# Which queue loads what, one held load, and the order of the first matmuls in a kernel that sums a state-space layer and a feed-forward layer

## The chip, the cores and the metric

The kernel runs on one core of a Trainium2 chip. The metric is the time of one execution on the device, in microseconds (us). TensorE (PE) does the matmuls, VectorE (DVE) and ScalarE (ACT) the elementwise work, GpSimd (POOL) some small operations and a few transfers. SyncE (SP) and ScalarE issue most of the transfers (DMAs), each into a queue of its own; 16 DMA engines carry all of them.

## What is computed

```python
xn = _layernorm(x)                                   # x: [1, 2048, 512], bf16
out = x + A(xn) + B(xn)

def A(x, ...):                                       # state-space layer, P = D = 512
    Lam_bar = exp(dt * Lam)                          # dt = exp(log_dt), Lam complex
    B_bar = ((Lam_bar - 1.0) / Lam)[:, None] * Bmat
    Bu = einsum("bld,pd->blp", x, B_bar)
    h_t = Lam_bar * h_{t-1} + Bu[:, t, :]            # over 2048 steps
    return 2.0 * einsum("blp,dp->bld", h, Cmat).real + x * Dskip

def B(x, w_gate, w_up, w_down):                      # F = 1376
    return (silu(x @ w_gate) * (x @ w_up)) @ w_down
```

## The kernel before

The 2048 rows of x are 16 tiles of 128 rows (`xall[:, n, :]`, called x0, x1, ... here), in four chunks of 512 rows. For each chunk TensorE needs the normalized rows transposed, `xnT` (512 features on partitions in four blocks `k`, rows as columns). Then come three kinds of matmuls: `bproj` (L346, the input of the recurrence, weights `BT`, eight groups of four), gate and up (L421, eleven feature tiles of 128 columns, weights `wg`, `wu`), and the output (`out_ffn` L501 and `out_ssm` L510, which add into the same PSUM bank). VectorE runs the recurrence as a scan (L388) between two complex rotations; ScalarE copies matmul results out of PSUM and does the silu.

The order of instructions on each engine is written out by hand (`manual_schedule`); a small backlog (`queue`, `pump`) interleaves the VectorE work of the recurrence with the matmul groups from the second chunk on. Waits between engines follow from the data. A DMA issued from SyncE or ScalarE uses one of eight completion semaphores in turn and, in the built program, waits until the DMA that had it before has landed.

The first chunk is done in a head of its own, tile by tile, because its loads arrive one after another:

- `dummy(11, CW)`: eleven matmuls of 512 columns on a constant, whose results are not used (L569), then TensorE waits for tile 0.
- VectorE: statistics of x0 (`ln_stats(0)`, L174 and L175), statistics of x1 (L600), the normalization of tile 0 (`norm_dve(0)`, L192), the second step of the statistics of x1 (L602), and so on, in this order. The reciprocal square root of the variance comes from ScalarE as `Ln` and `Exp` (`rstd_act`, L179 and L180), for which `preload_act_table_set` loads ScalarE's table (L596).
- `xT_pe(n)`: four transposes of tile n on TensorE (L209), in two halves of two feature blocks; ScalarE (L218) or VectorE (L216) copies each half to `xnT`. It is called T(n) in the prediction. After T(0) come four short dummies of 128 columns.
- `head_mm(which, lo, hi, ks, fis)` (L592): gate (`which` = 0) or up (1) matmuls for the row tiles `lo` to `hi`, feature blocks `ks` and feature tiles `fis`; feature tiles 0 and 1 first, since the first group of weights (`wg0`, `wu0`) holds these two. The results are kept in six PSUM banks until all four row tiles of the chunk are done.

The weights of gate and up come in four groups, `wg0` to `wg3` and `wu0` to `wu3` (two, two, three and three feature tiles; `load_w1`, L112). SyncE issues x0, wg0, x2, wg1, then x4 to x7 as one load (L126), wg2, wu2, four transposing loads of B's real part (`BT`, L131), wg3, wu3, four of its imaginary part, and three pieces of the last feature tile. ScalarE issues x1, wu0, x3, wu1. GpSimd issues three small parameter rows (`prm_rows`, L125).

The last feature tile has 96 columns (1280 to 1375). `w_last` packs its 96 gate columns and 32 of its up columns into one set of 128 weights; the other 64 up columns are in `wu_last`. The gate columns stand there in the order 1312 to 1375, 1280 to 1311, and `wd_sb` holds the matching rows of `w_down` in the same order, in two loads.

In the last chunk the result is added up on VectorE (L513) and stored per tile of 128 rows from SyncE (L514); only the last tile is cut into three column blocks, two of which ScalarE stores.

Of the kernel before, what the change touches and what calls it, by code (L numbers as in the profile page):

```python
# [10 lines left out]
F32 = mybir.dt.float32  # L11
# [12 lines left out]
def kernel(  # L24
# [17 lines left out]
    nc = tc.nc  # L42
    _, L, D = A_x.shape
    Pst = A_Lambda_re.shape[0]
    F = B_w_gate.shape[1]
    assert L % 512 == 0 and D % 128 == 0 and Pst % 128 == 0 and Pst == D
    CW = 512
# [3 lines left out]
    TPC = CW // 128  # L51
    KD = D // 128
# [6 lines left out]
    LA, LB = 32, 64  # L59
    FL = (FT - 1) * 128  # L60
    assert fsz[-1] == LA + LB and NCH % 2 == 0
    EPS = 1e-5

    const = ctx.enter_context(tc.tile_pool(name="const", bufs=1))
# [14 lines left out]
    x_v = A_x[0].rearrange("(n p) d -> p n d", p=128)  # L79
    out_v = out[0].rearrange("(n p) d -> p n d", p=128)  # L80
    wg_v = B_w_gate.rearrange("(k p) f -> p k f", p=128)
    wu_v = B_w_up.rearrange("(k p) f -> p k f", p=128)


    xall = const.tile([128, NT, D], BF16, name="xall")
# [3 lines left out]
    wg_g, wu_g = [], []  # L89
# [4 lines left out]
    w_last = const.tile([128, KD, 128], BF16, name="w_last")  # L94
    wu_last = const.tile([128, KD, LB], BF16, name="wu_last")
    wd_sb = const.tile([128, FT, D], BF16, name="wd_sb")
# [7 lines left out]
    def wslice(groups, fi, k):  # L104
        for (a, b), t in zip(fgroups, groups):
            if a <= fi < b:
                return t[:, k, (fi - a) * 128:(fi - a) * 128 + fsz[fi]]


    def load_w1(q, tiles, view, gi):  # L110
        a, b = fgroups[gi]
        q.dma_start(out=tiles[gi][:], in_=view[:, :, a * 128:min(F, b * 128)])  # L112


    nc.sync.dma_start(out=xall[:, 0, :], in_=x_v[:, 0, :])
    nc.scalar.dma_start(out=xall[:, 1, :], in_=x_v[:, 1, :])
    load_w1(nc.sync, wg_g, wg_v, 0)
    load_w1(nc.scalar, wu_g, wu_v, 0)
    nc.sync.dma_start(out=xall[:, 2, :], in_=x_v[:, 2, :])
    nc.scalar.dma_start(out=xall[:, 3, :], in_=x_v[:, 3, :])  # L120
    load_w1(nc.sync, wg_g, wg_v, 1)
    load_w1(nc.scalar, wu_g, wu_v, 1)
    prm_rows = const.tile([3 * NQ, 128], BF16, name="prm_rows")
    for i, v in enumerate((A_Lambda_re, A_Lambda_im, A_log_dt)):
        nc.gpsimd.dma_start(out=prm_rows[i * NQ:(i + 1) * NQ, :], in_=v.rearrange("(q j) -> q j", j=128))  # L125
    nc.sync.dma_start(out=xall[:, TPC:2 * TPC, :], in_=x_v[:, TPC:2 * TPC, :])  # L126
    load_w1(nc.sync, wg_g, wg_v, 2)
    load_w1(nc.sync, wu_g, wu_v, 2)
    for part, src in enumerate((A_B_re, A_B_im)):
# [3 lines left out]
            load_w1(nc.sync, wg_g, wg_v, 3)  # L133
            load_w1(nc.sync, wu_g, wu_v, 3)

    nc.sync.dma_start(out=w_last[:, :, 0:LB], in_=wg_v[:, :, FL + LA:F])
    nc.sync.dma_start(out=w_last[:, :, LB:LB + LA], in_=wg_v[:, :, FL:FL + LA])
    nc.sync.dma_start(out=w_last[:, :, LB + LA:128], in_=wu_v[:, :, FL:FL + LA])

    def load_late():  # L140
        nc.sync.dma_start(out=wu_last[:], in_=wu_v[:, :, FL + LA:F])
        nc.sync.dma_start(out=xall[:, 2 * TPC:NT, :], in_=x_v[:, 2 * TPC:NT, :])
        nc.sync.dma_start(out=wd_sb[:, 0:nfull, :], in_=B_w_down[0:nfull * 128, :].rearrange("(k p) d -> p k d", p=128))
        if nfull < FT:
            nc.sync.dma_start(out=wd_sb[0:LB, nfull, :], in_=B_w_down[FL + LA:F, :])
            nc.sync.dma_start(out=wd_sb[LB:LB + LA, nfull, :], in_=B_w_down[FL:FL + LA, :])

    nfull = F // 128


    ones = nc.const_aps.tensor(1.0, (128, CW), BF16)
    neg_half = const.tile([128, TPC], F32, name="neg_half")
    nc.vector.memset(neg_half[:], -0.5)
    eps_t = const.tile([128, 1], F32, name="eps_t")
    nc.vector.memset(eps_t[:], EPS)
    ident = const.tile([128, 128], BF16, name="ident")
    make_identity(nc, ident[:])
    jidx = const.tile([128, CW], F32, name="jidx")
# [14 lines left out]
    def ln_stats(n):  # L173
        nc.vector.bn_stats(out=stats[:, n, :], in_=xall[:, n, :])  # L174
        nc.vector.bn_aggr(out=mv[:, n, :], in_=stats[:, n, :])  # L175

    def rstd_act(n):

        nc.scalar.activation(out=ve[:, n:n + 1], in_=mv[:, n, 1:2], func=ACT.Ln, bias=eps_t[:, 0:1])  # L179
        nc.scalar.activation(out=rstd[:, n:n + 1], in_=ve[:, n:n + 1], func=ACT.Exp, scale=-0.5)  # L180
# [19 lines left out]
    HK = KD // 2  # L200

    def xT_pe(n, on_dve=(), prm_too=False):

        c, i = divmod(n, TPC)
        for h in range(2):
            tp = bank((128, HK * 128 + 3 * NQ), BF16)
            for k in range(HK):
                lo = (h * HK + k) * 128
                nc.tensor.transpose(out=tp[:, k * 128:(k + 1) * 128], in_=xn_tile(c)[:, i, lo:lo + 128],  # L209
                                    identity=ident[:])  # L210
            if prm_too and h == 1:
                prm_transpose(tp[:, HK * 128:])
            dst = xnT[:, h * HK:(h + 1) * HK, n * 128:(n + 1) * 128]
            src = tp[:, 0:HK * 128].rearrange("p (k t) -> p k t", k=HK)
            if h in on_dve:
                nc.vector.tensor_copy(out=dst, in_=src)  # L216
            else:
                nc.scalar.copy(out=dst, in_=src)  # L218
        return tp[:, HK * 128:]
# [270 lines left out]
    def out_blocks(n):  # L490

        return ((0, D // 2), (D // 2, D - 128), (D - 128, D)) if n == NT - 1 else ((0, D),)
# [11 lines left out]
    def out_ssm(n):  # L504
        c, i = divmod(n, TPC)
        res = opool.tile([128, D], BF16, name="res")
        for o, (lo, hi) in zip(o_tiles[n], out_blocks(n)):
            for part in range(2):
                for q in range(NQ):
                    nc.tensor.matmul(o[:], lhsT=w_tiles[c][:, part, q, i * 128:(i + 1) * 128],  # L510
                                     rhs=CF[:, part, q, lo:hi], start=False, stop=(part == 1 and q == NQ - 1))
            if c == NCH - 1:
                V.tensor_tensor(out=res[:, lo:hi], in0=o[:], in1=xn_end[:, i, lo:hi], op=ALU.add)  # L513
                (nc.sync if hi == D else nc.scalar).dma_start(out=out_v[:, n, lo:hi], in_=res[:, lo:hi])  # L514
            else:
                nc.scalar.copy(out=res[:, lo:hi], in_=o[:])  # L516
                nc.gpsimd.dma_start(out=out_v[:, n, lo:hi], in_=res[:, lo:hi], accum_op=ALU.add)  # L517
# [49 lines left out]
    def dummy(n, cols):  # L567
        for _ in range(n):
            nc.tensor.matmul(warm[:, 0:cols], lhsT=ones[:, 0:128], rhs=ones[:, 0:cols], start=True, stop=True)  # L569
# [18 lines left out]
    def head_mm(which, lo, hi, ks, fis):  # L588

        for fi in fis:  # L590
            for k in ks:
                nc.tensor.matmul(held[fi][which][:, lo * 128:hi * 128], lhsT=wslice((wg_g, wu_g)[which], fi, k),  # L592
                                 rhs=xnT[:, k, lo * 128:hi * 128], start=(k == 0), stop=(k == KD - 1))

    allk = range(KD)
    nc.scalar.preload_act_table_set("natural_log_exp_and_others")  # L596
    dummy(11, CW)
    ln_stats(0)
    rstd_act(0)
    nc.vector.bn_stats(out=stats[:, 1, :], in_=xall[:, 1, :])  # L600
# [6 lines left out]
    ln_stats(2)  # L607

    head_mm(0, 0, 1, range(0, HK), (0, 1))
    head_mm(1, 0, 1, range(0, HK), (0, 1))  # L610
    xT_pe(1)
    rstd_act(2)
    head_mm(0, 0, 1, range(HK, KD), (0, 1))
    head_mm(1, 0, 1, range(HK, KD), (0, 1))
    nc.vector.bn_stats(out=stats[:, 3, :], in_=xall[:, 3, :])
    norm_dve(2)
# [45 lines left out]
    def out_chunk(c):  # L662

        multiply(0)
        for n in range(c * TPC, (c + 1) * TPC):
            out_ffn(n)
            pump(FT * 0.2163)
        need(f"ssm{c}")
        need("cf")
        for n in range(c * TPC, (c + 1) * TPC):  # L670
            out_ssm(n)
            pump(2 * NQ * 0.2163)
# [28 lines left out]
    spread(fwd0[8:] + back0, norm2, "ssm0", "ln2")  # L701
    queue("cf", c_ops())
    load_late()
    for fi in range(G0, FT):
        gateup_tile(0, fi)
# [60 lines left out]
```

## Time and profile before

| | us |
|---|---|
| median of 3 runs | 180.13 |
| lowest and highest | 180.0, 180.2 |
| the profiled execution, whole | 180.19 |
| its span (first to last instruction) | 178.4 |

| engine | busy us | share of the span |
|---|---|---|
| TensorE, matmuls | 174.8 | 98% |
| TensorE, weight loads (beside matmuls) | 83.4 | 47% |
| VectorE | 153.1 | 86% |
| ScalarE | 93.9 | 53% |
| GpSimd | 23.2 | 13% |

All times of the trace count from the start of the span. The 1.8 us between the span and the whole lie before and after it. A line of the timeline has the start, the duration, the engine, the line of the kernel, the operation, what it writes and reads, and in brackets how long the engine was idle before it and what ended that. A "q" behind an engine's name is its queue issuing a transfer; the landing of the transfer is listed apart, in the issues, as us from the issue. The ends of matmuls are modelled, so the distance from one start to the next tells more of a matmul's pace than its own duration. The chain of waits is followed back from the last instruction to what released each step.

### The profile page before, as it was taken

Reading aid. Unit: us, or ns where it says so; the run is one execution under the profiler, and the core shown is the slowest. Engines: PE = TensorE matmul, PEld = TensorE weight load, DVE = VectorE, ACT = ScalarE, POOL = GpSimd, SP = SyncE. Lnnn points to the kernel's source line nnn. Section 1 sums busy time; section 2 is a strip of 40 time slices with the busy share of each in tenths; the row PEclk is TensorE's granted clock in tenths of the full one; section 3 lists DMA queues with packets and bytes.
Section 4 is the critical chain, followed back from the end, with each engine's and each line's share of the span. In section 5 each row is a group of like instructions: output and inputs, shape, how many; then the busy total and the mean of one; then the engine's idle time right before and its main releaser. Section 6 shows DMA issues by size and latency. Waiting matters only on the chain.

```text
span 178.4 us, 2463 instructions
## 1 busy us (share of the span) xinstructions
PE 174.8 (98%) x918; PEld 83.4 (47%) x918; DVE 153.1 (86%) x232; ACT 93.9 (53%) x173; POOL 23.2 (13%) x29
## 2 busy tenths in 40 slices
PE   8999999999999999999999999999999999999993
PEld 2784444444444444444444444444444444444743
DVE  2889996999999999999999999999999999950033
ACT  2579795988299957022998661024866610220000
POOL 6003000000500000027200000013405000150000
PEclk9999999999999999999999999999999999999999
DMA  5998657994137400020930000007096900072012
GB/s 169 313 256 235 114 104 190 359 160 109 34 63 235 180 0 0 0 29 6 131 75 0 0 0 0 4 0 87 9 139 90 146 5 0 0 85 32 4 48 70
DMA packets 29515, 15.53 MB, mean 87 GB/s; under 512 B 18336, under 2 KB 29440, under 8 KB 29472
## 3 DMA queue, kind: packets, MB, share of 16 engines
q1 hardware_dynamic: 24416, 11.21, 27.1%
q0 software_dynamic: 3456, 3.28, 13.8%
q10 hardware_dynamic: 1632, 0.89, 1.8%
q8 instruction: 7, 0.11, 0.3%
q14 instruction: 4, 0.03, 0.1%
HBM read 8.03 MB, written 5.24 MB: 74 GB/s over the span
## 4 chain that ended last, share of the span: by engine, by line
PE 98%; DVE 0%; issue 0%
PE ps L421 36%; PE ps L501 21%; PE ps L510 16%; PE ps L346 15%; PE ps L592 3%; PE ps L569 3%; PE ps L447 2%; PE ps L457 1%; PE ps L209 1%; DVE res L513 0%; PE ps L239 0%
## 5 line engine op out<-in xcount | busy, mean ns | idle before, releaser
L501 PE MATMUL ps<-wd_sb,guT 128*128 128x512 bf16 (+3 forms) x198 | 38.8, 356 | 0.0
L421 PE MATMUL ps<-xnT,wg 128*128 128x512 bf16 x148 | 38.0, 380 | 0.0
L421 PE MATMUL ps<-xnT,wu 128*128 128x512 bf16 x148 | 38.0, 379 | 0.0
L388 DVE TENSOR_TENSOR_SCAN g<-r_t,car,u 128x512 bf16<-128x512 f32 x24 | 28.9, 1267 | 0.0
L510 PE MATMUL ps<-CF,wt 128*128 128x512 bf16 (+2 forms) x144 | 28.3, 356 | 0.0
L346 PE MATMUL ps<-xnT,BT 128*128 128x512 bf16 x128 | 28.3, 379 | 0.0
L501 PEld LDWEIGHTS <-guT 128*128 128x128 bf16 (+1 forms) x198 | 18.5, 98 | 19.9
L516 ACT CAST res<-ps 128x512 bf16<-128x512 f32 x12 | 7.0, 585 | 38.0 <-PE ps L510 38.0
L435 ACT ACTIVATE guT<-ps 128x512 bf16<-128x512 f32 x40 | 24.9, 623 | 3.5 <-PE ps L421 3.4
L436 ACT CAST u<-ps 128x512 bf16<-128x512 f32 x40 | 24.3, 607 | 3.9 <-PE ps L421 3.9
L421 PEld LDWEIGHTS <-wu 128*128 128x128 bf16 x148 | 14.5, 98 | 17.5
L421 PEld LDWEIGHTS <-wg 128*128 128x128 bf16 x148 | 14.3, 98 | 17.6 <-issue 0.8
L517 POOL DMA_DIRECT2D out_dram<-res x12 | 11.1, 998 | 86.4 <-ACT res L516 86.4
L510 PEld LDWEIGHTS <-wt 128*128 128x128 bf16 x144 | 13.4, 98 | 14.3
L346 PEld LDWEIGHTS <-BT 128*128 128x128 bf16 x128 | 12.5, 98 | 15.1
L348 ACT CAST u<-ps 128x512 bf16<-128x512 f32 x32 | 17.4, 591 | 2.8 <-PE ps L346 2.7
L513 DVE TENSOR_TENSOR res<-ps,xn_end 128x512 bf16<-128x512 f32 (+2 forms) x6 | 3.0, 514 | 14.2 <-PE ps L510 14.2
L440 DVE TENSOR_TENSOR guT<-guT,u 128x1024 bf16<-128x1024 bf16 x20 | 13.5, 681 | 0.0
L174 DVE BATCH_NORM_STATS2 stats<-xall 128x6 f32<-128x512 bf16 x14 | 9.4, 670 | 2.6 <-DMA xall<-in_A_x_dram 2.6
L356 DVE TENSOR_TENSOR pm<-u,c 128x2048 bf16<-128x2048 bf16 x8 | 9.8, 1221 | 1.2 <-ACT c L273 1.1
L184 POOL TENSOR_TENSOR rstd<-ve,neg_half 128x4 f32<-128x4 f32 x3 | 5.3, 1750 | 41.9 <-DVE ve L183 41.9
L356 DVE TENSOR_TENSOR pm<-g,c 128x2048 bf16<-128x2048 bf16 x8 | 9.7, 1218 | 0.1
(102 smaller groups left out, 159.0 us busy)
## 6 DMA issues: line engine op xcount, KB each, us to landing
out_dram<-in_A_x_dram SPq DMA_DIRECT2D x1, 1536.0 KB, 8.0
out_dram<-res POOLq DMA_DIRECT2D x12, 128.0 KB, 3.1
out_dram<-xall POOLq DMA_DIRECT2D x3, 512.0 KB, 5.7
wd_sb<-in_B_w_down_dram SPq DMA_DIRECT2D x1, 1280.0 KB, 10.6
xall<-in_A_x_dram SPq DMA_DIRECT2D x1, 1024.0 KB, 6.2
wg<-in_B_w_gate_dram SPq DMA_DIRECT2D x2, 384.0 KB, 5.6
wu<-in_B_w_up_dram SPq DMA_DIRECT2D x2, 384.0 KB, 5.4
wu<-in_B_w_up_dram ACTq DMA_DIRECT2D x2, 256.0 KB, 5.1
```

The costliest lines, as they stand in the source:

```text
L174: nc.vector.bn_stats(out=stats[:, n, :], in_=xall[:, n, :])
L346: nc.tensor.matmul(ps[:], lhsT=BT[:, part, k, q * 128:(q + 1) * 128], rhs=xnT[:, k, c * CW:(c + 1) * CW], start=(k == 0), stop=(k == KD - 1))
L348: nc.scalar.copy(out=u_tiles[c][:, part, q, :], in_=ps[:])
L356: V.tensor_tensor(out=t[:], in0=flat(src()[:, i]), in1=flat(tab[:]), op=ALU.mult)
L388: V.tensor_tensor_scan(out=g()[:, part, q, :], data0=r_t[:, q:q + 1].to_broadcast([128, CW]), data1=u_tiles[c][:, part, q, :], initial=ini ...
L421: nc.tensor.matmul(ps[:fs, lo:hi], lhsT=wslice(groups, fi, k), rhs=xnT[:, k, c * CW + lo:c * CW + hi], start=(k == 0), stop=(k == KD - 1))
L435: nc.scalar.activation(out=guT[:fs, fi, :], in_=psg[:fs], func=ACT.Silu)
L436: nc.scalar.copy(out=u_pair[c][:fs, fi % 2, :], in_=psu[:fs])
L440: products.append(lambda: V.tensor_tensor(out=g, in0=g, in1=u, op=ALU.mult))
L501: nc.tensor.matmul(o[:], lhsT=gu_tiles[c][:fsz[fi], fi, i * 128:(i + 1) * 128], rhs=wd_sb[:fsz[fi], fi, lo:hi], start=(fi == 0), stop=False)
L510: nc.tensor.matmul(o[:], lhsT=w_tiles[c][:, part, q, i * 128:(i + 1) * 128], rhs=CF[:, part, q, lo:hi], start=False, stop=(part == 1 and q ...
L517: nc.gpsimd.dma_start(out=out_v[:, n, lo:hi], in_=res[:, lo:hi], accum_op=ALU.add)
```

## The change

- SyncE issues x0, wg0, wu0, wg1, wu1; ScalarE issues x1, x2, x3. A VectorE memset writes half of x1's buffer first; the load of x1 overwrites it and so waits for it.
- The two small memsets that stood further down on VectorE, and the load of ScalarE's table, now stand ahead of these loads.
- x4 to x7 come in two loads of two tiles.
- Nine long dummies instead of eleven.
- For row tile 0, all four blocks of gate come first, then T(1), then all four blocks of up. Before, T(1) stood between blocks 0 and 1 of gate and up and blocks 2 and 3.
- The last feature tile's columns stay in order: `w_last` comes in two loads, its rows of `w_down` in one. The numbers of matmuls stay as they were.
- The first of the four stores of the last chunk is cut into two halves of 256 columns, from ScalarE and SyncE.

```diff
+    neg_half = const.tile([128, TPC], F32, name="neg_half")
+    nc.vector.memset(neg_half[:], -0.5)
+    eps_t = const.tile([128, 1], F32, name="eps_t")
+    nc.vector.memset(eps_t[:], EPS)
+
+    nc.scalar.preload_act_table_set("natural_log_exp_and_others")
+
     nc.sync.dma_start(out=xall[:, 0, :], in_=x_v[:, 0, :])
+    nc.vector.memset(xall[:, 1, 0:D // 2], 0.0)
     nc.scalar.dma_start(out=xall[:, 1, :], in_=x_v[:, 1, :])
     load_w1(nc.sync, wg_g, wg_v, 0)
-    load_w1(nc.scalar, wu_g, wu_v, 0)
-    nc.sync.dma_start(out=xall[:, 2, :], in_=x_v[:, 2, :])
+    nc.scalar.dma_start(out=xall[:, 2, :], in_=x_v[:, 2, :])
+    load_w1(nc.sync, wu_g, wu_v, 0)
     nc.scalar.dma_start(out=xall[:, 3, :], in_=x_v[:, 3, :])
     load_w1(nc.sync, wg_g, wg_v, 1)
-    load_w1(nc.scalar, wu_g, wu_v, 1)
+    load_w1(nc.sync, wu_g, wu_v, 1)
...
-    nc.sync.dma_start(out=xall[:, TPC:2 * TPC, :], in_=x_v[:, TPC:2 * TPC, :])
+    for n in (TPC, TPC + 2):
+        nc.sync.dma_start(out=xall[:, n:n + 2, :], in_=x_v[:, n:n + 2, :])
...
-    nc.sync.dma_start(out=w_last[:, :, 0:LB], in_=wg_v[:, :, FL + LA:F])
-    nc.sync.dma_start(out=w_last[:, :, LB:LB + LA], in_=wg_v[:, :, FL:FL + LA])
-    nc.sync.dma_start(out=w_last[:, :, LB + LA:128], in_=wu_v[:, :, FL:FL + LA])
+    nc.sync.dma_start(out=w_last[:, :, 0:LB + LA], in_=wg_v[:, :, FL:F])
+    nc.sync.dma_start(out=w_last[:, :, LB + LA:128], in_=wu_v[:, :, FL + LB:F])
...
-        nc.sync.dma_start(out=wu_last[:], in_=wu_v[:, :, FL + LA:F])
+        nc.sync.dma_start(out=wu_last[:], in_=wu_v[:, :, FL:FL + LB])
...
-            nc.sync.dma_start(out=wd_sb[0:LB, nfull, :], in_=B_w_down[FL + LA:F, :])
-            nc.sync.dma_start(out=wd_sb[LB:LB + LA, nfull, :], in_=B_w_down[FL:FL + LA, :])
+            nc.sync.dma_start(out=wd_sb[0:F - FL, nfull, :], in_=B_w_down[FL:F, :])
...
-                (nc.sync if hi == D else nc.scalar).dma_start(out=out_v[:, n, lo:hi], in_=res[:, lo:hi])
+                for a, b in ((0, D // 2), (D // 2, D)) if i == 0 else ((lo, hi),):
+                    (nc.sync if b == D else nc.scalar).dma_start(out=out_v[:, n, a:b], in_=res[:, a:b])
...
-    nc.scalar.preload_act_table_set("natural_log_exp_and_others")
-    dummy(11, CW)
+    dummy(9, CW)
...
     head_mm(0, 0, 1, range(0, HK), (0, 1))
-    head_mm(1, 0, 1, range(0, HK), (0, 1))
+    head_mm(0, 0, 1, range(HK, KD), (0, 1))
     xT_pe(1)
     rstd_act(2)
-    head_mm(0, 0, 1, range(HK, KD), (0, 1))
+    head_mm(1, 0, 1, range(0, HK), (0, 1))
     head_mm(1, 0, 1, range(HK, KD), (0, 1))
```

More of the change, by code (lines that the diff above doesn't have):

```diff
@@ L144, in load_late @@
         if nfull < FT:
-            nc.sync.dma_start(out=wd_sb[0:LB, nfull, :], in_=B_w_down[FL + LA:F, :])
-            nc.sync.dma_start(out=wd_sb[LB:LB + LA, nfull, :], in_=B_w_down[FL:FL + LA, :])
+            nc.sync.dma_start(out=wd_sb[0:F - FL, nfull, :], in_=B_w_down[FL:F, :])
     nfull = F // 128
     ones = nc.const_aps.tensor(1.0, (128, CW), BF16)
[L152 to L155, printed above, removed]
     ident = const.tile([128, 128], BF16, name="ident")
```

## Prediction

> **What bounds the kernel now.** I read the chain of waits first, then the timeline of the first 14 us, then the DMA issues one by one, then DMA rates by window. The chain in order of time:
>
> ```profile
> 0.78 4.85 PE ps L569 x11
> 5.63 0.31 PE ps L209 x4
> 5.94 0.23 PE ps L569 x4
> 6.17 0.04 issue
> 6.21 0.61 PE ps L592 x8
> ...
> 175.60 0.02 issue
> 175.63 0.29 DVE res L513
> ```
>
> TensorE is the chain from end to end. Past 6.21 us the idle in it is 0.02 us, so later loads, VectorE work and stores are covered, and what an edit is worth is how far it moves the start of that stream. Up to 5.63 the stream is eleven dummy matmuls (L569) that compute nothing. What releases the first real work is in the timeline:
>
> ```profile
> 0.74 0.41 ACTq L116 DMA_DIRECT2D xall<-in_A_x_dram  x1
> 0.74 0.40 SPq L115 DMA_DIRECT2D xall<-in_A_x_dram  x1
> ...
> 2.78 1.28 ACT L596 ACT_TABLE_LOAD   x1 [2.78 <-issue]
> ...
> 3.55 0.69 DVE L174 BATCH_NORM_STATS2 stats<-xall 128x6 f32<-128x512 bf16 x1 [2.65 <-DMA xall<-in_A_x_dram]
> ...
> 4.37 0.66 DVE L600 BATCH_NORM_STATS2 stats<-xall 128x6 f32<-128x512 bf16 x1
> ...
> 5.06 0.41 DVE L192 TENSOR_SCALAR xall<-xall,mv,rstd 128x512 bf16<-128x512 bf16 x1
> ...
> 5.52 0.25 PEld L209 LDWEIGHTS <-xall 128*128 128x128 bf16 x4 [0.80 <-DVE xall L192]
> ```
>
> The transposes of tile 0 wait for its normalization (L192), that for the statistics (L174), those for the landing of tile 0 (x0) at 3.5. Statistics of tile 1 (L600) stand in front of L192 on VectorE, so x1 counts too. The dummies start 0.427 us apart (last one at 5.00), so the eleventh is through at 5.43, just before L192 ends at 5.47: both edges meet. The head thus hangs on x0's landing, then on x1's. The issues that started together:
>
> ```profile
> xall<-in_A_x_dram ACTq DMA_DIRECT2D x1, 128.0 KB, 3.0
> xall<-in_A_x_dram SPq DMA_DIRECT2D x1, 128.0 KB, 2.8
> ```
>
> x0 and x1, on two queues in the same instant, land 2.8 and 3.0 us later: they share the engines. Read in the same way one by one: wg0 lands 3.7 after its issue at 1.20 (4.9), wu0 4.2 after 1.18 (5.4), x2 4.6 after 1.66 (6.3), x3 5.1 after 1.67 (6.8), wg1 5.9 after 2.21 (8.1), wu1 6.0 after 2.29 (8.3).
>
> **The change, part by part.** *x0 alone.* In the windows the engines go from 70 GB/s (2.00 to 2.25) to 324 to 336 GB/s (2.25 to 3.00). x1's 131 KB at 332 GB/s is 0.39 us of shared transfer taken out from before x0's end: x0 lands at 3.1 instead of 3.5, gain 0.39. Bounds: no gain, if x0's 2.8 us is latency and not share; at most 0.7, since the quickest load on the page from a quiet queue (wu_last, 64 KB) lands 2.1 us after issue. I take 0.39, nearest to the row of these very loads.
>
> *The hold.* x1 now waits for a memset of half of it, third on VectorE after 0.84 + 0.06. VectorE's tiny memsets take 0.06, GpSimd's 128x128 one 0.22: x1 is issued at 1.0 to 1.15. By its own row it lands 3.0 later, 4.0 to 4.15; by x0's, 2.8, 3.8 to 3.95. L600 wants it at 4.37 - 0.39 = 3.98. Loss 0 to 0.17; I take 0.05, since x1 now shares with wg0 and has nothing before it on its queue. Behind it on ScalarE's queue are x2 and x3: issued at about 1.55 and 2.0, wanted at 6.48 and 7.30 less the gain. Half the bytes ahead of them are gone (wu0 left the queue), so they should land by 5.0 and 5.8.
>
> *The table load* moves from 2.78 to the front of ScalarE, 0.75 to 2.03. It must be done by L179 (4.49, then 4.1); at the old place it ended at 4.06. Worth nothing, if it does not hold back the DMAs behind it (a rival below).
>
> *wu0 and wu1 to SyncE, gate of tile 0 first.* The PE now does gate k0 to k3 of feature tiles 0 and 1, then T(1), then up. The second half of xnT, copied by ScalarE until 6.38, is wanted at 6.43 instead of 6.88: at most 0.02 late. wu0 is now wanted at 6.83 - 0.3 = 6.5 instead of 6.38. Ahead of its end are x0 to x3, wg0 and itself, 1.05 MB. By the windows (about 611 KB by 4.0, 767 by 4.5, 897 by 5.0, 1030 by 5.5) that much is moved by 5.6; loads land 0.4 to 0.8 after their bytes (wg0 and wu0), so 6.0 to 6.4. Loss 0; if the lag is 1.2 us, as for x3, wu0 lands at 6.8 and costs 0.3. wg1 and wu1 have the same bytes ahead as before, or fewer.
>
> *Eleven dummies to nine.* The ninth ends at 0.78 + 9 x 0.427 = 4.62. It removes 0.85 us of blocking in front of transposes that now want to start at 5.53 - 0.32 = 5.2. Left at eleven, they would end at 5.43 and eat 0.2 of the gain. So it gains nothing of its own, and leaves PE idle for about 0.6 us.
>
> *The rest, at nothing.* x4 to x7 in two loads: one more SyncE issue (0.4 to 0.5). SyncE's second half now waits for wg0 (each load reuses the semaphore of the one eight before), then wu2 for wu0. BT's first transpose, at 5.82 now, goes out near 6.7, 0.9 later; the BT, wg3 and wu3 loads behind it follow. The last BT transpose (issued 18.25, landing 2.9 later) comes at 22.0 instead of 21.15. Its first reader is the fourth matmul of the fifth group of four at L346, 19.40 + 19 x 0.216 = 23.5, less 0.3: 1.2 us of cover. If that is gone it costs one for one. w_last in two loads takes one issue of 0.5 out again, so the transposes of chunk 1 (21.36 to 26.5, landing 2.4 later) keep their cover to 32.35, and one wd_sb load of 0.63 goes too. The last feature tile has the same matmuls in another row order: 0. The extra ScalarE store of tile 12 goes out at 171.1, while the end hangs on L513 at 175.63: 0.
>
> Sum: 0.39 - 0.05 - 0.02 = 0.32 us less. The profiled execution took 180.19 (span 178.4): 179.87. The median of the runs is 180.13: 179.81, so 179.8.
>
> **The rivals.** *A: the table load holds x1.* Nothing in this trace has a ScalarE DMA behind running ScalarE work. For it: the table load started at 2.78, just after the last issue there ended (2.29 + 0.46), so the queue goes in order. Against: the profile books issues and computation on separate rows, and on SyncE issues go out back to back. If held, x1 goes out at 0.75 + 1.28 = 2.03, lands 3.0 later at 5.03, L600 ends at 5.69, and L192 starts there, not at 5.06: 0.6 slower, 180.8; it decides as soon as x1 is issued after 1.5. The Trainium skill (Perfetto Trace Analysis, Sequencer Loop) says that a sequencer pushes an engine instruction into a queue and reads on; by that rule x1 is not held and this rival falls. No row here shows it.
>
> *B: the clock.* The dummies start 0.427 us apart, at 4.15, 4.57 and 5.00; later 128x512 matmuls run at 0.216 (6.91 us for 32 in the chain), although the page's granted clock reads 1.00 throughout. So TensorE doubled its pace between 5.0 and 5.53, that is 4.2 to 4.7 us after its first matmul. If the 0.6 us of idle starts that count anew at 5.2, it stays slow until 9.4 or later, and the work from 5.9 to 9.4 takes twice as long: 1.75 us lost, less 0.32: 181.6. If the doubling only comes late by the idle time, 0.1 to 0.2 us goes. Against: the idle is a sixth of the 3.8 us of dummies. The Trainium skill (TensorE: Matmul & The Clock Gate, Part 1) has the pace set by a free-running window of about 3.4 us that must be busy, and this speaks against fewer dummies: a window with a hole in it may not open the gate. By that page a whole window would be lost, about 1.7 us as an estimate, where the rows give 1.75.
>
> *C: more.* x0 takes what a quiet load takes: 2.1 to 2.3 us. Landing at 2.84 to 3.04 and x1 by 3.6: gain 0.5 to 0.7, 179.5. For it: x0 is then the only load. Against: 128 KB, not 64.
>
> *D: nothing.* x0's time is latency, or wu0 or x1 comes late by 0.3: 180.1.
>
> **How the numbers follow.** The forecast (gain 0.15 to 0.55) 0.55; A 0.13, B 0.12, C 0.13, D 0.07. A difference under 0.2%, 0.36 us, can't be told from none in this kernel. Half of the forecast's range lies past that, and all of C: faster 0.27 + 0.13 = 0.40. Same: 0.28 + 0.07 = 0.35, rounded down to 0.34. Slower: A and B, 0.25, rounded up to 0.26. The forecast alone runs from 179.55 to 180.0. The range for 8 in 10 goes from 179.4 (C) to 180.8 (A), and leaves out B and the ends of A and C.
>
> **What would show it.** x0 landing at 3.1 and L174 starting there; x1 issued at 1.0 to 1.15 while the table load runs; L600 straight after the first aggregate; tile 0's transposes at about 5.2 after idle from 4.62; the first up matmuls without a wait for wu0; then the same chain 0.3 earlier everywhere, with no idle near 23 us. Wrong if x1 is issued after 2.0 (A), if L592's 128-column matmuls start a quarter of 0.427 us apart, 0.107, and not a quarter of 0.216 (B), or if x0 still lands at 3.5 (D).

## The result, and the profile after

| | before | after |
|---|---|---|
| median us (lowest to highest, runs) | 180.22 (179.93 to 180.58, 22) | 179.91 (179.57 to 180.69, 22) |
| ratio to before, 95% interval | | 0.9982 (0.9975 to 0.9989) |
| the profiled execution, whole | 180.19 | 179.99 |
| its span | 178.4 | 178.2 |

The median is 0.31 us (0.18%) lower, beside a forecast of 179.8. The interval lies below 1, so the gain is small but clear of the scatter of these runs; it stays under the 0.2% that the prediction took as the least that can be told from none.

The chain of waits of the changed kernel (start us, us, what), cut to its head and its last piece:

```profile
0.74 2.21 DMA xall<-in_A_x_dram
...
2.98 0.70 DVE stats L178
...
3.89 0.59 DVE stats L604
4.47 0.01 issue
4.49 0.42 DVE xall L196
4.91 0.05 issue
4.95 0.61 PE ps L213 x4
5.56 0.43 PE ps L574 x4
5.99 0.68 PE ps L597 x8
6.66 0.22 PE ps L213 x4
...
175.47 0.29 DVE res L517
```

The chain no longer begins with eleven dummies but with the landing of x0, at 2.95. The transposes of tile 0 (L213; called T(0) here) begin at 4.95, 0.57 earlier than before (5.52). Yet the last VectorE operation is only 0.16 earlier (175.47 against 175.63). The loss lies in the first 1.7 us of the stream: the timeline of the changed kernel shows it.

```profile
0.74 1.28 ACT L120 ACT_TABLE_LOAD   x1 [0.74 <-PEq L754]
1.10 0.43 ACTq L125 DMA_DIRECT2D xall<-in_A_x_dram  x1
...
4.95 0.34 PEld L213 LDWEIGHTS <-xall 128*128 128x128 bf16 x4 [1.08 <-DVE xall L196]
...
5.25 0.47 PEld L574 LDWEIGHTS <-const-bfloat16-1.0 128*128 128x128 bf16 x4
...
5.67 0.81 PEld L597 LDWEIGHTS <-wg 128*128 128x128 bf16 x8
...
6.45 0.27 PEld L213 LDWEIGHTS <-xall 128*128 128x128 bf16 x4
```

Take the weight loads (PEld), which start when a group can start: from T(0) to T(1), with four short dummies and eight gate matmuls in between, it is 4.95 to 6.45, 1.50 us. Before, the same four transposes, four dummies and eight matmuls took from 5.52 to 6.62, 1.10 us. So 0.40 of the 0.57 went into slower matmuls: four short dummies take 0.47 us here, four transposes at 6.45 only 0.27. TensorE reached its full pace shortly before 6.45, while the granted clock in the profile reads 1.00 in every half microsecond from 3 to 6.5. After that nothing else is lost or won: TensorE waits for nothing from 7 to 175 us, in the window of the moved BT transposes (20 to 26 us) it is busy 6.00 of 6.00 us, and from the end of the last VectorE operation to the end of the span it is 2.45 us (2.49 before; the page rounds the span, in the trace it is 178.41 before and 178.21 after).

The first issues of the changed kernel, one by one (what, queue, size, us from issue to landing):

```profile
xall<-in_A_x_dram SPq DMA_DIRECT2D x1, 128.0 KB, 2.2
xall<-in_A_x_dram ACTq DMA_DIRECT2D x1, 128.0 KB, 2.3
wg<-in_B_w_gate_dram SPq DMA_DIRECT2D x1, 256.0 KB, 3.4
wu<-in_B_w_up_dram SPq DMA_DIRECT2D x1, 256.0 KB, 4.8
```

x0 lands 2.2 after its issue, not 2.8; x1 (issued at 1.10) lands at 3.4, before VectorE wants it (3.80); wu0, issued at 1.65 as the third load on SyncE, at 6.45.

### The profile page after: what moved, and what is told of

Its sections match the earlier page's. It is cut to its first block, busy times and chain, and to the rows that moved or that the text cites. A ratio compares the mean times of both kernels' runs of the same rounds, so it can differ in the third digit from the quotient of the medians.

```text
span 178.2 us, 2462 instructions
## 1 busy us (share of the span) xinstructions
PE 174.5 (98%) x916; PEld 83.8 (47%) x916; DVE 153.1 (86%) x233; ACT 94.3 (53%) x173; POOL 23.2 (13%) x29
## 4 chain that ended last, share of the span: by engine, by line
PE 96%; DMA 1%; DVE 1%; issue 0%
PE ps L425 36%; PE ps L505 21%; PE ps L514 16%; PE ps L350 16%; PE ps L597 3%; PE ps L451 2%; DMA xall<-in_A_x_dram 1%; PE ps L461 1%; PE ps L213 1%; DVE stats L178 0%; DVE stats L604 0%; PE ps L574 0%; DVE xall L196 0%; DVE res L517 0%; DVE mv L179 0%
```

## The experiments

Each kernel below was profiled once and timed beside the kernel before on the same chip; the ratio is to that. A profile shows one execution, so a landing read from it may differ in the next. "The end" means the time from the end of the last VectorE operation to the end of the span.

### The changed kernel again

No edit; a second profile of the same program.

> The changed kernel once more, unaltered, to see what differs from one execution to the next. If the time at which TensorE doubles its pace belongs to the execution and not to the kernel, the 0.15 us weight loads end at another time than 6.3 in this profile; the time is again 179.9, 0.3 below the kernel before. If the hole after nine dummies sets it, it is 6.3 again.

Measured: 179.79 (179.62 to 180.02), ratio 0.9977 (0.9968 to 0.9986). Its timeline, TensorE's weight loads:

```profile
4.88 0.23 PEld L213 LDWEIGHTS <-xall 128*128 128x128 bf16 x4 [1.03 <-DVE xall L196]
...
5.98 0.24 PEld L213 LDWEIGHTS <-xall 128*128 128x128 bf16 x4
...
6.72 0.34 PEld L597 LDWEIGHTS <-wu 128*128 128x128 bf16 x6 [0.50 <-DMA wu<-in_B_w_up_dram]
```

Here TensorE has its full pace well before 4.88: the last two dummies start at 3.72 and 3.96, 0.24 apart and no longer 0.43. T(0) to T(1) takes 1.10. Now the up matmuls wait 0.50 for wu0, which lands at 6.7. The last VectorE operation is at 175.42, almost where it was in the first profile (175.47). So two different losses give the same time: a slow TensorE hides that wu0 is late, a quick one waits for it. When the pace doubles differs between executions of the same program.

### Ten and eleven dummies

```diff
-    dummy(9, CW)
+    dummy(10, CW)   # d11: dummy(11, CW)
```

> The changed kernel with ten long dummies. They end at 0.78 + 10 x 0.427 = 5.05, 0.1 after the transposes could start at 4.95, so TensorE never idles. Theory 1: full pace (0.10 us weight loads) by 5.5; the first gate matmuls follow the copies of xnT at about 5.75 and T(1) comes at about 6.15 to 6.2, not at 6.50: 0.3 below the changed kernel, 179.6. Theory 2: pace as random as with nine, transposes 0.1 later: 179.9 to 180.0.

> The changed kernel with eleven long dummies again, all else as changed. Theory 1 (the hole between the last dummy and tile 0's transposes keeps TensorE at half pace longer): weight loads take 0.10 us, not 0.15, from the transposes on; these start where the eleventh dummy ends, 5.43 to 5.48, so about 0.5 later than with nine, but nothing after them is slow: about 180.15, 0.05 to 0.1 below the kernel before. Theory 2 (the pace doubles at a time of its own, whatever the dummies do; 6.3 in one profile and under 5.5 in the other by chance): the profile shows 0.15 us loads until some other time, and the run is slower than before by as much as in the other runs, 180.2 to 180.5.

Measured: with ten 179.78 (179.68 to 180.25), ratio 0.9975 (0.9965 to 0.9985); with eleven 180.20 (179.64 to 180.52), 0.9987 (0.9976 to 0.9998). The timeline with eleven:

```profile
5.00 0.15 PEld L213 LDWEIGHTS <-xall 128*128 128x128 bf16 x1 [0.28 <-DVE mv L606]
5.43 0.55 PE L213 MATMUL ps<-ident,xall 128*128 128x128 bf16 x4
5.43 0.36 PEld L213 LDWEIGHTS <-xall 128*128 128x128 bf16 x3 [0.28 <-issue]
```

Tile 0's first weights are in at 5.00, but the matmuls start only when the eleventh dummy is through, at 5.43: that is 0.48 later than with nine. With ten, T(0) starts at 4.90, at full pace (T(1) at 6.00), and the first up matmuls wait 0.25 for wu0. Ten and nine cannot be told apart in time, so the idle that nine dummies leave (4.62 to 4.95) costs nothing as a rule. With eleven there is no idle, and T(0) still ran partly at half pace.

### Nine dummies in the kernel before

```diff
-    dummy(11, CW)
+    dummy(9, CW)
```

> The kernel before with nine long dummies, nothing else. The transposes still start at 5.5, since x0 lands as before; TensorE idles from 4.62 to 5.5. Theory 1: weight loads take 0.15 us until 6.3 or later, the matmuls of the head are late: 0.2 to 0.6 slower than before, 180.4 to 180.8. Theory 2: same as before, 180.2.

Measured: 180.16 (179.98 to 181.99), ratio 1.0004 (0.9984 to 1.0025). T(0) moved from 5.52 to 5.20 at full pace after idle from 4.62, but in this execution wg0 landed 4.7 us after issue (3.7 before) and wu0 5.4 (4.2), and the first gate and up matmuls waited 0.24 and 0.53 for them. x0 had landed 0.33 earlier than in the profile before (3.19 against 3.52), which the edit does not touch, so the earlier T(0) is not the work of the edit alone. Fewer dummies alone show no gain: the loads are next in line. Two of the twelve executions took 181.57 and 181.99; no trace shows why.

### x1 not held

```diff
-    nc.vector.memset(xall[:, 1, 0:D // 2], 0.0)
```

> The changed kernel without the memset of x1's buffer, so x1's load is issued with x0's at 0.74. If the hold is what lets x0 land early (2.2 us after its issue), x0 lands 2.8 us after its issue again, its statistics start at 3.5 and the transposes at 5.5: 0.5 late, partly paid back since TensorE may be at full pace by then; about 180.2 to 180.5. If x0 lands early because of the other changes of the load order (wu0 gone from ScalarE's queue), x0 still lands at about 2.95 and the time is that of the changed kernel, 179.9.

Measured: 180.13 (179.79 to 182.05), ratio 1.001 (0.9986 to 1.0033); two of eleven executions took 181.65 and 182.05, again without a trace. Its timeline, and the issue of wg0:

```profile
5.04 0.23 PEld L212 LDWEIGHTS <-xall 128*128 128x128 bf16 x4 [1.17 <-DVE xall L195]
...
5.96 0.45 PEld L596 LDWEIGHTS <-wg 128*128 128x128 bf16 x8 [0.46 <-DMA wg<-in_B_w_gate_dram]
```

```profile
wg<-in_B_w_gate_dram SPq DMA_DIRECT2D x1, 256.0 KB, 4.7
```

x0 still lands at 2.3 after issue, 0.1 later than with the hold, though x1 is now issued 0.04 us after it and not 0.36. Going by this one profile, sharing with x1 is not what kept x0 at 2.8 in the kernel before. What the hold protects is wg0: 4.7 us instead of 3.4 (without a hold wg0 took 3.7, 4.1 and 4.7 in the three profiles with the loads of before; with it 3.2 to 3.6 in ten). All of ScalarE's loads stand behind the held one, so with it x2 and x3 are issued 0.35 later too (1.55 and 2.04 against 1.20 and 1.68). That wg0 is quicker because it shares less is argued and not shown. The gate matmuls wait 0.46 without it. By medians the hold is worth 0.15 to 0.35 us (180.13 against 180.28 before on this chip, where ten dummies took 179.78; the changed kernel 179.91 against 180.22), though the wide interval doesn't exclude less.

### The order of the first matmuls as before

```diff
     head_mm(0, 0, 1, range(0, HK), (0, 1))
-    head_mm(0, 0, 1, range(HK, KD), (0, 1))
+    head_mm(1, 0, 1, range(0, HK), (0, 1))
     xT_pe(1)
     rstd_act(2)
-    head_mm(1, 0, 1, range(0, HK), (0, 1))
+    head_mm(0, 0, 1, range(HK, KD), (0, 1))
     head_mm(1, 0, 1, range(HK, KD), (0, 1))
```

> The changed kernel with the first matmuls in the order of before (gate and up of blocks 0 and 1, T(1), gate and up of blocks 2 and 3). wu0 is the third load of SyncE now and lands at 6.4 to 6.5; in this order the up matmuls want it at 5.9 to 6.1 and T(1) stands behind them. If gate first is what makes the late wu0 bearable: T(1) comes at 6.7 instead of 6.1 to 6.5, about 0.3 slower than the changed kernel, 180.2. If the order is worth nothing: 179.9.

Measured: 180.27 (180.0 to 180.63), ratio 1.0002 (0.9993 to 1.001). The timeline:

```profile
6.45 0.23 PEld L597 LDWEIGHTS <-wu 128*128 128x128 bf16 x4 [0.68 <-DMA wu<-in_B_w_up_dram]
...
6.63 0.27 PEld L213 LDWEIGHTS <-xall 128*128 128x128 bf16 x4
```

The up matmuls come ahead of T(1), wait 0.68 for wu0, and T(1) waits behind them. Without the new order the whole gain is gone: gate first is what pays for wu0's place on SyncE.

### The edits behind the head alone

The kernel before with three of the change's edits, and no other:

```diff
-    nc.sync.dma_start(out=xall[:, TPC:2 * TPC, :], in_=x_v[:, TPC:2 * TPC, :])
+    for n in (TPC, TPC + 2):
+        nc.sync.dma_start(out=xall[:, n:n + 2, :], in_=x_v[:, n:n + 2, :])
...
-    nc.sync.dma_start(out=w_last[:, :, 0:LB], in_=wg_v[:, :, FL + LA:F])
-    nc.sync.dma_start(out=w_last[:, :, LB:LB + LA], in_=wg_v[:, :, FL:FL + LA])
+    nc.sync.dma_start(out=w_last[:, :, 0:LB + LA], in_=wg_v[:, :, FL:F])
...
-            nc.sync.dma_start(out=wd_sb[0:LB, nfull, :], in_=B_w_down[FL + LA:F, :])
-            nc.sync.dma_start(out=wd_sb[LB:LB + LA, nfull, :], in_=B_w_down[FL:FL + LA, :])
+            nc.sync.dma_start(out=wd_sb[0:F - FL, nfull, :], in_=B_w_down[FL:F, :])
...
-                (nc.sync if hi == D else nc.scalar).dma_start(out=out_v[:, n, lo:hi], in_=res[:, lo:hi])
+                for a, b in ((0, D // 2), (D // 2, D)) if i == 0 else ((lo, hi),):
+                    (nc.sync if b == D else nc.scalar).dma_start(out=out_v[:, n, a:b], in_=res[:, a:b])
```

> The kernel before with only the edits behind the head: x4 to x7 in two loads, the last feature tile in order, the first store of the last chunk in two halves. All of these lie beside other work: same as before, 180.2 to 180.3, and TensorE starts L346 and L501 at the same distance from the head as before. If one of them counts, the time is off by 0.2 or more and a new idle stretch shows in the chain.

Measured: 180.44 (180.22 to 180.76), ratio 1.001 (1.0001 to 1.0019). The chain of waits of this run:

```profile
2.21 6.45 DMA wg<-in_B_w_gate_dram
8.65 0.05 issue
8.70 0.61 PE ps L592 x4
```

In this execution, the slowest of the eleven, TensorE waits for wg1, which lands at 8.66 (8.1 before). wg1 is issued at 2.21, ahead of everything that these edits touch, so this wait need not be theirs. The end took 2.64, 0.15 more than before. So these edits gain nothing alone, and probably lose a little (0.22 in the medians).

### x3 behind wu0 on SyncE, ten dummies

```diff
-    nc.scalar.dma_start(out=xall[:, 3, :], in_=x_v[:, 3, :])
+    nc.sync.dma_start(out=xall[:, 3, :], in_=x_v[:, 3, :])
...
-    dummy(9, CW)
+    dummy(10, CW)
```

> The changed kernel with ten long dummies and with x3 loaded by SyncE behind wu0 instead of by ScalarE. In the run with ten dummies the first up matmuls waited 0.25 us for wu0, which landed at 6.45 behind 1.05 MB of other loads. Without x3 (0.13 MB) in front it should land 0.3 to 0.4 earlier, and x3, now last, near 6.5, just before it is wanted (6.7). If wu0 is what bounds the head then: 0.2 below ten dummies alone, about 179.6. If x3 becomes late instead: the normalization of tile 2, which stands behind x3's statistics on VectorE, is late by as much, and the time is that of ten dummies, 179.8, or above.

Measured: 180.18 (179.96 to 180.67), ratio 1.0001 (0.9991 to 1.0011). wu0 landed at 6.05 as hoped for, and the last VectorE operation was at 175.52, near that of the changed kernel. But the end took 2.95 us, not 2.45. This was a loss that nobody had priced, and the next three kernels look for it.

### x3 on SyncE, with one issue more there, and with none more

The first kernel has only the move of x3, with nine dummies. The second has in addition x4 to x7 in one load again, so that SyncE issues as many transfers as in the changed kernel: 50 by the list of issues, against 51.

```diff
-    nc.scalar.dma_start(out=xall[:, 3, :], in_=x_v[:, 3, :])
+    nc.sync.dma_start(out=xall[:, 3, :], in_=x_v[:, 3, :])
...
-    for n in (TPC, TPC + 2):
-        nc.sync.dma_start(out=xall[:, n:n + 2, :], in_=x_v[:, n:n + 2, :])
+    nc.sync.dma_start(out=xall[:, TPC:2 * TPC, :], in_=x_v[:, TPC:2 * TPC, :])
```

> The changed kernel with x3 moved from ScalarE to SyncE, behind wu0; nothing else, nine dummies, x4 to x7 in two loads. SyncE has one instruction more than in the changed kernel. If the longer end comes with the one instruction more on SyncE, it is there again: 2.9 to 3.0 us after the last VectorE operation, time 180.1 to 180.3, and 0.4 to 0.5 above the run that has x4 to x7 in one load. If it was chance of one execution: 2.45, and 179.6 to 179.9. wu0 lands near 6.05 in both cases.

> The changed kernel with x3 moved from ScalarE to SyncE, behind wu0, and x4 to x7 in one load again, so that SyncE issues as many transfers as in the changed kernel and ScalarE one fewer. Nine dummies. The run with x3 on SyncE behind wu0 and ten dummies had wu0 at 6.05 instead of 6.45, the same start of the stream, and 2.99 us after the last VectorE operation where others have 2.45; 0.5 of that lay between two drains of SyncE at the end. Theory (the end is longer because SyncE has one instruction more, so that what stands at its end is placed otherwise): here the end is back at 2.45 and the time is 179.6 to 179.8. Rival (the end is longer because ScalarE has one transfer fewer, or because of x3 itself): the end is 2.9 to 3.0 again and the time is 180.1 to 180.3.

Measured: with 51 issues 180.15 (179.94 to 180.66), ratio 0.9998 (0.9989 to 1.0007); with 50 179.85 (179.55 to 179.99), 0.9977 (0.9967 to 0.9986). In the profile of the run with 51 the last VectorE operation is at 175.06, 0.41 earlier than in the changed kernel, and yet the span is 0.1 longer: the end takes 2.98. With 50 it takes 2.59. Where the time is, by SyncE's own records at the program's last line (operation, count, shortest/median/longest ns, first and last start) in slices of 0.1 us of the run with 51 (a DRAIN is one of the closing instructions there):

```profile
L765 SPq DRAIN  x1: 13/13/13, 177.0 to 177.0; - x1
L765 SPq DRAIN  x1: 114/114/114, 177.5 to 177.5; - x1
```

And the same of the changed kernel, both drains in one slice:

```profile
L765 SPq DRAIN  x2: 7/7/7, 177.3 to 177.4; - x2
```

In the changed kernel the first two drains follow each other at once. With one issue more, 0.5 us pass between them and the second takes 114 ns instead of 7; no DMA or engine releases it in the trace.

### The head's edits without the ones behind it

The changed kernel with the diff of "the edits behind the head alone" taken back: x4 to x7 in one load, the last feature tile as before (three loads of `w_last`, two of `wd_sb`'s last rows), the first store whole. SyncE then has 51 issues, and x3 is back on ScalarE.

> The changed kernel with four of its edits undone: x4 to x7 in one load, the last feature tile's columns in the order of before (three loads of w_last, two of wd_sb's last rows), the first store of the last chunk whole. The loads at the start, the held x1, nine dummies and the order of the first matmuls stay. SyncE issues one transfer more than in the kernel before and in the changed kernel, as in the two runs with x3 on SyncE, which lost 0.5 us between two drains at the end. Theory (one instruction more on SyncE costs 0.5 at the end, wherever it is): 2.9 to 3.0 us after the last VectorE operation, and 180.1 to 180.4, though the stream starts as in the changed kernel; then the edits to the last feature tile, priced at nothing, are worth 0.3 to 0.5 because they take back the issue that the others add. Rival (the longer end belongs to x3 on SyncE): 2.45 and 179.7 to 179.95.

Measured: 180.44 (180.08 to 180.61), ratio 1.0008 (0.9999 to 1.0017). The stream starts as in the changed kernel (4.94), the last VectorE operation is at 175.39, and the end takes 2.96:

```profile
L765 SPq DRAIN  x1: 13/13/13, 177.3 to 177.3; - x1
...
L765 SPq DRAIN  x1: 114/114/114, 177.8 to 177.8; - x1
```

The same gap, without x3 on SyncE. All three kernels with 51 issues have it (ends of 2.95, 2.98 and 2.96), and none of the ten profiles with 50 (2.45 to 2.59). ScalarE has five issues instead of six in these three, but also in the kernel with x4 to x7 in one load, whose end is 2.59. That the long end goes with the count on SyncE is shown. The kernel with 49 issues (the edits behind the head alone) had 2.64, so it is not a saving per issue. Two of its records (L761), and the one behind the first two drains of the changed kernel (L765), tell more:

```profile
L761 SPq EVENT_SEMAPHORE  x1: 17/17/17, 178.2 to 178.2; - x1
L761 SPq DRAIN  x1: 114/114/114, 178.7 to 178.7; - x1
...
L765 SPq EVENT_SEMAPHORE  x1: 17/17/17, 177.9 to 177.9; - x1
```

With 49 issues there is a gap of 0.5 us too, and a drain of 114 ns behind it, but it is the third drain. In the changed kernel, with 50, the gap lies between the second drain (177.39) and the semaphore instruction behind it (177.89). Counted through SyncE's records in the trace, from the first one on, the gap is between the 79th and the 80th in all fourteen profiles, 0.48 to 0.51 us long. So one issue more does not add a pause: it moves the closing instructions by one place against a pause that is always there. With 50 the pause falls beside GpSimd's own work at the last line, which runs until 177.92 in the changed kernel, and is nearly hidden: from the first drain to the end of the span it is 0.87 us, against 1.05 with 49 and 1.35 with 51. What makes the pause stays open.

### wu0 on ScalarE, x2 on SyncE

```diff
-    nc.scalar.dma_start(out=xall[:, 2, :], in_=x_v[:, 2, :])
-    load_w1(nc.sync, wu_g, wu_v, 0)
+    nc.sync.dma_start(out=xall[:, 2, :], in_=x_v[:, 2, :])
+    load_w1(nc.scalar, wu_g, wu_v, 0)
```

> The changed kernel with wu0 and x2 exchanged between the queues: ScalarE issues x1 (still held), wu0, x3; SyncE issues x0, wg0, x2, wg1, wu1. Each queue issues as many transfers as in the changed kernel. Ahead of the end of wu0 now stand x0, x1, wg0 and part of x2, about 0.2 MB less than before, at 330 GB/s 0.5 us or so. Theory (wu0, third on SyncE, is what the gain is given back to): wu0 lands near 5.9 to 6.1 and not at 6.5 to 6.7, the first up matmuls wait for nothing where TensorE has its full pace by 4.9, the stream starts 0.3 to 0.5 earlier than in the unchanged kernel, and the time is 179.3 to 179.6, ratio 0.995 to 0.9965. Where TensorE still runs at half pace until 6.3, 0.1 or less is gained. Rival (the two queues share the engines evenly and wu0 on ScalarE then takes from wg0): wg0 lands at 5.6 to 5.9 instead of 4.6 to 4.8, the first gate matmuls wait 0.3 or more, and the time is 180.0 to 180.3. Second rival: x2, now behind wg0, is late, and the second pair of row tiles waits.

Measured: 179.64 (179.52 to 179.74, 5 runs), ratio 0.9967 (0.9955 to 0.9979): the fastest kernel of the study, 0.61 us below the kernel before. The changed kernel's ratios are 0.9982 and 0.9977, so against it the gain is 0.1% to 0.15%, and the intervals overlap. The timeline:

```profile
4.96 0.23 PEld L213 LDWEIGHTS <-xall 128*128 128x128 bf16 x4 [1.09 <-DVE xall L196]
...
6.06 0.24 PEld L213 LDWEIGHTS <-xall 128*128 128x128 bf16 x4
6.26 0.49 PEld L597 LDWEIGHTS <-wu 128*128 128x128 bf16 x8
```

TensorE has its full pace at 4.96, as in the second profile of the changed kernel; but wu0 now lands 4.2 after its issue at 1.55, at 5.80, and the up matmuls follow T(1) without a wait. wg0 still lands 3.4 after issue, so the rival (wu0 takes from wg0) did not come true. x2 was not late (5.60), but x3 was (6.96), and VectorE waited 0.17 for it. The last VectorE operation is at 175.19, 0.23 before that of the second profile. The wait of 0.50 is gone from the trace; that wu0's place on SyncE held back part of the gain is borne out by it, while the times of five runs alone would not show it.

## Why the prediction was right

The forecast of 0.32 us less met 0.31 in the medians. That the two agree so closely is luck: the start of the stream moved by 0.57 and not by 0.34, then TensorE's pace in one profile and the wait for wu0 in the other, neither of them in the sum, took a good part of it back, and the mechanism of the largest term is not borne out.

- **x0 alone, +0.39.** The size was in the range, the mechanism given is not borne out. Against the one profile before, the gain is 3.55 - 2.98 = 0.57. That profile was at the late end: with the same first loads x0's statistics started at 3.22 with nine dummies and at 3.43 in the run of the later edits. With x0 alone at first they started between 2.83 and 3.02 in all ten profiles. So 0.2 to 0.7, and 0.39 is well inside. But the prediction drew the 0.39 from x1's 131 KB, taken out from before x0's end. Without the hold these bytes are back: x1's first packet starts at 2.04 and x0's last at 2.57, and yet the statistics started at 3.06, 0.04 past the ten. By this the hold is worth 0.04 to 0.23 to x0. What brought the rest is open: the other loads (wu0 no longer second on ScalarE), the earlier table load, or the scatter between executions, since there is one profile without the hold.
- **The hold, -0.05.** x1 was issued at 1.10, as worked out, and landed 2.3 later and not 2.8 to 3.0: the rows of loads that shared the engines were the wrong ones for it. No loss. What the prediction did not price is the other effect of the hold: with it wg0 lands 3.2 to 3.6 us after issue, without it 3.7 to 4.7.
- **The table load (A)** fell: x1's DMA was issued on ScalarE at 1.10, in the middle of the table load (0.74 to 2.02). The Trainium skill (Perfetto Trace Analysis, Sequencer Loop) says that the sequencer pushes an engine instruction into a queue and reads on, and the trace agrees with that.
- **Gate first and wu0 on SyncE, -0.02.** The step "Loss 0; if the lag is 1.2 us, as for x3, wu0 lands at 6.8 and costs 0.3" failed in its first half. wu0 landed at 6.45 and 6.7, not at 6.0 to 6.4, and with x0 earlier than priced TensorE wanted it at 6.22 in the second profile: a wait of 0.50. The bytes went as worked out, 1.05 MB by 5.5 in both profiles; what was too small was the lag behind them, 0.9 and 1.2 us and not 0.4 to 0.8. The bound was near the truth. In the profiled execution the wait is absent only since TensorE was slow.
- **Eleven dummies to nine, 0.** The prediction said eleven would eat 0.2 of the gain: T(0) starts 0.48 later with them (5.43 against 4.95), and the ratios differ by 0.0005 to 0.0012 from those with nine and ten, 0.1 to 0.2 us. In the first profile the idle is 0.33, not 0.6, since T(0) came earlier.
- **B (the clock)** did not come true as a rule. The changed kernel's profiles show T(0) to T(1) in 1.50 and in 1.10 us; nine dummies in other kernels gave 1.10, 1.23, 1.24 and 1.42, ten gave 1.10 and 1.57. It doesn't go with the idle. The Trainium skill (TensorE: Matmul & The Clock Gate, Part 1) has the pace set by a window of about 3.4 us that runs freely and does not start with the kernel, so that the point of change differs between runs; with that the trace agrees, 3.8 us into the span in one execution of the changed kernel and 6.3 in the other. Its length does not fit every profile: in the run of the later edits dummies started 0.22 apart from 3.56 on, 2.8 us after the first matmul of the span, sooner than one such window. Four of the 23 executions of the two kernels with nine dummies and no hold (nine dummies in the kernel before, x1 not held; TensorE's idle before T(0) is 0.44 and 0.55 us by their profiles) took 1.4 to 1.9 us more than their medians, near B's 181.6. Idle of that length is not enough for it: by the same account the second profile of the changed kernel has 0.54 and the run of the later edits 0.81, and none of their 21 executions took more than 180.76. Without a trace of a slow one the cause stays open.
- **The rest, at nothing.** Right for the change as a whole, and for a reason that the prediction did not have. Moving wu0 and wu1 to SyncE and x2 to ScalarE, and cutting x4 to x7, adds two issues to SyncE; the last feature tile in order takes two out; the count stays at 50. With the later edits undone it is 51, and the kernel is 0.5 us slower (180.44). The prediction had priced an issue at its 0.4 to 0.5 us in the queue, early and hidden, and not where it puts SyncE's pause at the end. The BT transposes kept their cover, as said, but not by the steps given: the first went out 1.06 later (6.88 against 5.82), the last as before (18.23 against 18.25), and it landed at 20.93 and not at 22.0.
- **C** was right about x0 (2.2 us from issue) and wrong about the time: TensorE's pace or wu0 took the surplus.

## What to carry over

When a load at the head is made faster, price the next load in line against the new, earlier moment at which it is wanted; here x0's 0.57 us became 0.2 to 0.3, and putting wu0 on the other queue brought part of the rest back. Take a second profile of the same program before explaining a gain by one: TensorE's pace at the start alone moved the head of this one by 0.40 us. And look at the end of the span as well as at the chain: one issue more on SyncE cost 0.5 us there, with all the work before it on time, because a pause of that length was no longer hidden.

## What the hardware showed that was not expected

- TensorE's change of pace came at 3.8 us into the span in one execution of a program and at 6.3 in another, and at 3.4 in another kernel with the same first matmuls; the granted clock in the profile (1.00) shows nothing of it. What shows it is the time of four short weight loads, 0.47 us at half pace and 0.27 after, or the distance of the long dummies, 0.43 and 0.22.
- About 0.5 us pass between the 79th and the 80th record of SyncE in every one of the fourteen profiles. With 50 issues this is hidden, with 51 it lies between the first two drains at the end of the program and the end is 0.5 us longer. The Trainium skill (Runtime: NRT & Kernel Launch, Instruction fetch mechanics) says that an engine fetches its instructions in blocks of 256 and that crossing into the next is mostly hidden. A block's edge at a fixed place among SyncE's instructions would look like this; no run here shows the fetch, so it remains a guess.
- Issuing ScalarE's first 128 KB load 0.32 us later (1.10 against 0.78) changed little for x0 (2.2 against 2.3 us), the load that it was to protect, but the 256 KB load that SyncE issued second landed 3.4 instead of 4.7 us after its issue. The second figure is from one profile; the spread without a hold is 3.7 to 4.7.
